# Linear attention's state as (phi(k)^T x) Wv, with phi(k) of all tokens kept and its sum made by GpSimd

## The chip, the cores and the metric

The kernel runs on one core of one Trainium2 chip. The metric is the device time of one launch in microseconds (us). The kernel before takes 493.31 us, the median of three runs (493.12 to 495.45).

## The reference

x is [2048, 1024] in bf16, with 32 heads of 32. Two attention blocks read the same x, and a gate mixes them per token:

```python
g = sigmoid((x * gate_w).sum(-1, keepdims=True))

# A: linear attention
q, k, v = split(x @ A_wqkv)
pq, pk = phi(q), phi(k)              # phi(t) = where(t > 0, t + 1, exp(t)) + 1e-6
kv  = einsum("bhsd,bhse->bhde", pk, v)        # the state: 32 x 32 for each head
z   = einsum("bhsd->bhd", pk)
num = einsum("bhqd,bhde->bhqe", pq, kv)
den = einsum("bhqd,bhd->bhq", pq, z)[..., None] + 1e-6
a   = (num / den) @ A_wo

# B: softmax over 8 keys, the token's own and those 2, 4, ... 14 back
b = window_attention(split(x @ B_wqkv)) @ B_wo

out = g * a + (1 - g) * b
```

B_x is not used. The state is a sum over all 2048 tokens, so nothing of A's output can be made before the last token's phi(k) is there.

## The kernel before

**Order of the work.** The builder writes down operations (engine, cost, what they read and write), and a planner (`Prog.schedule`) puts them in a fixed order for each engine before anything runs: it always takes the ready operation that was written down earliest, with costs that are written in the source. The chip then follows these orders; semaphores carry what one engine waits for from another. The planner runs six times and keeps the order that it finds shortest. In its model every engine works by itself. DMAs are started from SyncE (SP), in order.

**Stages.** Tokens are held in 16 tiles of 128, the even tokens first and then the odd ones, since the window of B steps by two.

1. B's values for all tokens (32 groups), stored to HBM. A *group* is 8 matmuls of 128x512 that fill one PSUM bank (L1323).
2. The gate.
3. B's q and k, transposed, into `qT` and `kT` (64 groups).
4. The *linear phase*: for each tile t, two groups of A's k and two of A's v. k goes through `phi` (L1327 to L1333): ScalarE's exp into `e` (L1329), VectorE's min and add on `e` (L1330), VectorE's max and add from PSUM (L1332). v is moved to SBUF by ScalarE or VectorE, whichever the planner finds free (`move`, L1347). The state of a tile is a *state burst* of 32 small matmuls (L1535: K = 128 tokens, 32 columns, N = 33, the 33rd column being ones, which gives z), and VectorE adds it to `kva` in SBUF (L1543).
5. *Fills*: the window attention of B runs inside stages 3 and 4, one fill of 112 or 114 tokens for every five groups (`slot(FILL)`, 18 fills in all). A fill is a scores burst (L1424), ScalarE's exp into `E` (L1430), VectorE's multiplication by the window's mask (L1433), and a values burst (L1443 and L1449) with its division: ScalarE's Ln and Exp (L1458, L1459), VectorE's product into `qT` (L1460). The scores and values share four PSUM banks; the groups have the other four.
6. `fold`: A's output matrix is multiplied by the state, head by head (L1573), in place in `ws[1]`. `z_spread` copies z to all partitions by two matmuls with ones (L1583).
7. For each tile: `query` (A's q and its phi), `scaled` (VectorE: q times z, sum per head, reciprocal, product; a DMA transposes the result into `kT`, L1610), and `output` (32 matmuls of 128x512, B's and A's part in one bank, L1626).

**SBUF.** `ws` are four weight slots of 16 KB per partition. Slot 1 and 2 hold B's Wk and Wq in stage 3, slot 3 A's Wk and slot 0 A's Wv in stage 4, slot 1 A's Wo and slot 2 A's Wq after that, slot 3 B's Wo.

**Around the change.** The linear phase is one loop over t with four groups each (L1545 to L1563). `states` holds a tile's state burst back by four slots. After the loop, the first queries follow, then `z_spread`, `scaled` and `fold` among queries and the first output (L1637 to L1666).

Of the kernel before, what the change touches and what calls it, by code (L numbers as in the profile page):

```python
# [7 lines left out]
ALU = mybir.AluOpType  # L8
AX = mybir.AxisListType
BF16 = mybir.dt.bfloat16  # L10
# [1092 lines left out]
def build_kernel(nc, A_x, A_wqkv, A_wo, B_x, B_wqkv, B_wo, gate_w, out):  # L1103
# [20 lines left out]

    rings = []
# [40 lines left out]
    ident = SB([128, 128], BF16, "ident")  # L1166
# [11 lines left out]
    kva = SB([128, 8, 33], F32, "kva")  # L1178
    kvb = SB([128, 8, 32], BF16, "kvb")
    kvT = SB([128, 8, 32], BF16, "kvT")  # L1180
    zdg = SB([128, 8, 128], BF16, "zdg")
# [5 lines left out]
    warm = SB([128, 512], BF16, "warm")  # L1187
    er = Ring([SB([128, 512], BF16, "e%d" % i) for i in range(3)])
# [16 lines left out]
    pk = Ring([SB([128, 1024], BF16, "pk%d" % i) for i in range(2)])  # L1205
    az = Ring([SB([128, H, 33], BF16, "az%d" % i) for i in range(2)])
# [3 lines left out]
    pnr = Ring([SB([128, 1024], BF16, "pn%d" % i) for i in range(2)])  # L1210
    base[0] = max(base[0], top_)
    pr = Ring([SB([128, 1024], BF16, "p%d" % i) for i in range(3)])
# [12 lines left out]
    def plan(seen):  # L1225
# [28 lines left out]
        C("pool", lambda e: e.memset(ident[:], 0.0), 0.2, [ident.all()])  # L1254
        C("pool", lambda e: e.affine_select(out=ident[:], in_=ident[:], compare_op=ALU.not_equal, fill=1.0, base=0,
                                            pattern=[[-1, 128]], channel_multiplier=1), 0.3, [ident.all()], [ident.all()])
# [211 lines left out]
        states = []  # L1468

        def slot(rate):  # L1470
            slot_n[0] += 1
            while later and later[0][0] <= slot_n[0]:
                later.pop(0)[1]()
            while states and states[0][0] <= slot_n[0]:
                states.pop(0)[1]()
# [42 lines left out]
        load_w(1, 0, Ao, 0, 40)  # L1518
        load_w(1, 1, Ao, 512, 41)
        load_w(2, 0, Aw, 0, 42)  # L1520
        load_w(2, 1, Aw, 512, 43)


        for z in az.t:
            P.op("pool", lambda e, z=z: e.memset(z[:, :, 32:33], 1.0), 0.2, writes=[z.part((0, H), (32, 33))])

        def state(t, pkt, azt):
            bank = main.next()

            def fn(e):  # L1530
                last = None
                for i in range(8):
                    for j in range(4):
                        h = 4 * i + j
                        last = e.matmul(bank.ap()[32 * j:32 * j + 32, i * 33:i * 33 + 33], pkt[:, h * 32:(h + 1) * 32], azt[:, h, :],  # L1535
                                        start=True, stop=True, tile_position=(0, 32 * j))
                return last
            P.op("pe", fn, 0.22, mode="c", reads=[pkt.all(), azt.all()], writes=[bank.iv], name="kv")
            src = lambda: bank.ap(0, 264).rearrange("p (i c) -> p i c", c=33)
            if t == 0:  # L1540
                P.op("dve", lambda e: e.tensor_copy(kva[:, :, :], src()), dps(264), reads=[bank.iv], writes=[kva.all()])
            else:
                P.op("dve", lambda e: e.tensor_tensor(kva[:, :, :], src(), kva[:, :, :], ALU.add), dps(264), reads=[bank.iv, kva.all()], writes=[kva.all()])  # L1543

        for t in range(NT):  # L1545
            pkt, _ = pk.next()
            azt, _ = az.next()
            xs, xr = x_tile(t)
            for r in range(4):
                bank = main.next()  # L1550
                w, wr = w_half((3, 0)[r // 2], r % 2)
                group(bank, xs, w, [xr, wr])
                if r < 2:
                    phi(bank, pkt[:, r * 512:(r + 1) * 512], pkt.part((r * 512, (r + 1) * 512)))
                else:
                    hh = (r - 2) * 16
                    dst = azt[:, hh:hh + 16, 0:32]
                    src = lambda bank=bank: bank.ap().rearrange("p (h d) -> p h d", d=32)
                    reg = azt.part((hh, hh + 16), (0, 33))
                    move(dst, src, 512, bank, reg)  # L1560
                if r == 3:
                    states.append((slot_n[0] + 4, lambda t=t, pkt=pkt, azt=azt: state(t, pkt, azt)))
                slot(FILL)  # L1563

        def fold(gq, jh):
            bs = [main.next() for _ in range(4)]
            w = ws[1].part((4 * gq, 4 * gq + 4), (jh * 512, jh * 512 + 512))

            def fn(e):
                for a in range(4):  # L1570
                    for j in range(4):
                        b = (a + j) % 4
                        last = e.matmul(bs[j].ap()[32 * b:32 * b + 32, :], kvT[32 * j:32 * j + 32, 4 * gq + b, :], ws[1][32 * j:32 * j + 32, 4 * gq + b, jh * 512:(jh + 1) * 512],  # L1573
                                        start=True, stop=True, tile_position=(32 * j, 32 * b))
                return last
            P.op("pe", fn, 0.45, mode="r", reads=[kvT.all(), w], writes=[b.iv for b in bs], name="fold")
            for j in range(4):
                move(ws[1][:, 4 * gq + j, jh * 512:(jh + 1) * 512], bs[j].ap, 512, bs[j], ws[1].part((4 * gq + j, 4 * gq + j + 1), (jh * 512, jh * 512 + 512)))

        def z_spread():  # L1580
            for hf in range(2):
                bank = main.next()
                P.op("pe", lambda e, hf=hf, bank=bank: e.matmul(bank.ap(), ones[:, :], zdg[:, 4 * hf:4 * hf + 4, :].rearrange("p i n -> p (i n)"), start=True, stop=True),  # L1583
                     mm(512), reads=[ones.all(), zdg.part((4 * hf, 4 * hf + 4), (0, 128))], writes=[bank.iv], name="z")
                move(zb[:, hf * 512:(hf + 1) * 512], bank.ap, 512, bank, zb.part((hf * 512, (hf + 1) * 512)))

        def query(t, r):
            p_ = pr.t[t % len(pr.t)]
            xs, xr = x_tile(t)
            bank = main.next()  # L1590
            w, wr = w_half(2, r)
            group(bank, xs, w, [xr, wr])
            phi(bank, p_[:, r * 512:(r + 1) * 512], p_.part((r * 512, (r + 1) * 512)))

        def scaled(t):
# [8 lines left out]
            for gq in range(2):  # L1604
# [5 lines left out]
            P.op("sp", lambda e: e.dma_start_transpose(kT[:, :, t * 128:(t + 1) * 128], pn[:, :]), 1.5, reads=[pn.all()],  # L1610
                 writes=[kT.part((0, 8), (t * 128, (t + 1) * 128))], chan="pn%d" % (t % 2), lat=1.3)

        def output(t, between=()):
            between = list(between)
# [3 lines left out]
            for f0, f1 in parts:  # L1618
# [4 lines left out]
                for lh, w, first in ((qT, ws[3], True), (kT, ws[1], False)):  # L1623
# [4 lines left out]
                    if not first and between:  # L1628
                        between.pop(0)()
# [7 lines left out]
        for t in range(2):  # L1637
            for r in range(2):
                query(t, r)
                slot(FILL)  # L1640
        while todo or later or states:
            slot(1.0)
        load_w(3, 0, Bo, 0, 50)
        load_w(3, 1, Bo, 512, 51)
        main = Pool(banks)
        P.op("dve", lambda e: e.tensor_copy(kvb[:, :, :], kva[:, :, 0:32]), 0.3, reads=[kva.all()], writes=[kvb.all()])
        P.op("dve", lambda e: e.transpose(kvT[:, :, :].rearrange("p i d -> p (i d)"), kvb[:, :, :].rearrange("p i d -> p (i d)")), 0.3, reads=[kvb.all()], writes=[kvT.all()])
        P.op("dve", lambda e: e.tensor_tensor(zdg[:, :, :], ident[:, None, :].to_broadcast([128, 8, 128]), kva[:, :, 32:33].to_broadcast([128, 8, 128]), ALU.mult),
             1.3, reads=[kva.all(), ident.all()], writes=[zdg.all()])
        query(2, 0)  # L1650
        query(2, 1)
        z_spread()
        scaled(0)
        query(3, 0)
        query(3, 1)
        fold(0, 0)
        output(0, [lambda: fold(1, 0), lambda: (scaled(1), query(4, 0), fold(0, 1), query(4, 1), fold(1, 1), scaled(2))])
        query(5, 0)
        query(5, 1)
        for t in range(1, NT):  # L1660
            if t + 2 < NT:
                scaled(t + 2)
            output(t)
            if t + 5 < NT:
                query(t + 5, 0)
                query(t + 5, 1)  # L1666
# [66 lines left out]
```

## Time and profile before

| | |
|---|---|
| median of 3 runs | 493.31 us (493.12 to 495.45) |
| profiled execution, its own time | 493.83 us |
| its span, first to last instruction | 490.9 us |
| TensorE busy | 477.2 us |
| VectorE / ScalarE / GpSimd busy | 288.5 / 150.8 / 5.1 us |
| granted TensorE clock | 1.00 |
| DMA moved | 39.09 MB |

A row of a timeline has the start in us from the span's start, the duration in us, the engine (PE is TensorE, PEld its weight loads, DVE VectorE, ACT ScalarE, POOL GpSimd), the source line, the operation, its output and input, the shape and how many were merged; in brackets, the idle time before it and what ended that. A row of a group gives the summed busy time, the mean in ns of one, and the idle time before. A row of waits gives the waiting engine and line, what it waited for, the total in us, how often, and the longest. Dense matmuls overlap: one has a duration of 379 ns, but the next starts about 215 ns after it, so the costs of work on TensorE are read from start to start. A few matmul records can be missing from a trace, so a count of x15 can stand for 16.

### The profile page before, as it was taken

How to read it: one execution, taken by the hardware profiler on the slowest of the kernel's cores; microseconds unless marked ns; L12 is line 12 of the kernel's file. 1: busy time of each engine (PE TensorE's matmuls, PEld its weight loads, DVE VectorE, ACT ScalarE, POOL GpSimd, SP SyncE). 2: the span in 40 equal slices, each digit the busy share in tenths (PEclk: the TensorE clock that was granted, in tenths of full speed). 3: DMA queues.
4: the chain of work that ended last, by engine and by line, in shares of the span. 5: the costliest groups of instructions: out<-in, count | busy, mean ns of one | idle time of the engine just before them, and what ended most of it. 6: DMA issues, size and time to landing. Idle time of an engine off the chain costs nothing.

```text
span 490.9 us, 11311 instructions
## 1 busy us (share of the span) xinstructions
PE 477.2 (97%) x5066; PEld 227.7 (46%) x5131; DVE 288.5 (59%) x486; ACT 150.8 (31%) x234; POOL 5.1 (1%) x27
## 2 busy tenths in 40 slices
PE   8999999999999999999999999999999999999996
PEld 3444444444444444455554545444444444444444
DVE  2122144655677777555664654579997777767522
ACT  2111111111344445466565556435322100011000
POOL 4000000000000000000000000000000000000000
PEclk9999999999999999999999999999999999999999
DMA  8989991000005045111100100501233311122111
GB/s 220 218 192 283 347 345 4 1 0 0 2 26 194 23 135 88 40 25 36 35 24 23 29 21 1 163 12 23 64 80 85 52 43 44 43 75 55 43 44 46
DMA packets 64176, 39.09 MB, mean 80 GB/s; under 512 B 39029, under 2 KB 59894, under 8 KB 64122
## 3 DMA queue, kind: packets, MB, share of 16 engines
q1 hardware_dynamic: 63578, 37.78, 29.3%
q8 instruction: 42, 0.69, 0.6%
q10 hardware_dynamic: 544, 0.52, 0.4%
q14 instruction: 12, 0.10, 0.1%
HBM read 21.51 MB, written 8.40 MB: 61 GB/s over the span
## 4 chain that ended last, share of the span: by engine, by line
PE 95%; SPq 2%; issue 2%; DMA 1%; DVE 0%
PE ps_all L1323 65%; PE ps_all L1626 22%; PE ps_all L1424 2%; PE ps_all L1443 2%; SPq L1293 1%; PE ps_all L1535 1%; DMA w<-in_B_wqkv_dram 1%; PE ps_all L1449 1%; SPq L1298 1%; PE ps_all L1387 0%; PE ps_all L1573 0%; DVE o L1353 0%; PE ps_all L1583 0%
## 5 line engine op out<-in xcount | busy, mean ns | idle before, releaser
L1323 PE MATMUL ps_all<-w,xT 128*128 128x512 bf16 x986 | 222.5, 379 | 6.0 <-issue 4.6
L1323 PEld LDWEIGHTS ps_all<-w,xT 128*128 128x128 bf16 x1024 | 97.2, 98 | 117.5 <-issue 2.0
L1323 PE MATMUL ps_all<-xT,w 128*128 128x512 bf16 x497 | 109.9, 379 | 1.7 <-issue 1.4
L1323 PEld LDWEIGHTS ps_all<-xT,w 128*128 128x128 bf16 x512 | 49.3, 98 | 58.8 <-issue 0.4
L1329 ACT ACTIVATE e<-ps_all 128x512 bf16<-128x512 f32 x64 | 38.2, 597 | 124.0 <-PE ps_all L1323 119.7
L1626 PE MATMUL ps_all<-w,kT 128*128 128x512 bf16 (+1 forms) x260 | 60.1, 372 | 0.2
L1626 PE MATMUL ps_all<-w,qT 128*128 128x512 bf16 (+1 forms) x256 | 59.8, 372 | 0.5 <-issue 0.2
L1330 DVE TENSOR_SCALAR e<-e 128x512 bf16<-128x512 bf16 x64 | 18.6, 290 | 40.8 <-ACT e L1329 40.5
L1626 PEld LDWEIGHTS ps_all<-w,kT 128*128 128x128 bf16 x264 | 25.8, 98 | 29.4
L1626 PEld LDWEIGHTS ps_all<-w,qT 128*128 128x128 bf16 x264 | 25.6, 98 | 29.6 <-issue 0.5
L1353 DVE TENSOR_SCALAR o<-ps_all,gm 128x512 bf16<-128x512 f32 (+1 forms) x28 | 20.5, 732 | 27.8 <-PE ps_all L1626 27.8
L1350 DVE CAST vst<-ps_all 128x512 bf16<-128x512 f32 x15 | 10.4, 692 | 43.9 <-PE ps_all L1323 43.9
L1430 ACT ACTIVATE E<-ps_all 128x1824 bf16<-128x1824 f32 (+1 forms) x18 | 30.4, 1687 | 11.7 <-PE ps_all L1424 11.0
L1279 DVE TENSOR_TENSOR mx<-mx,qT 128x1024 bf16<-128x1024 bf16 x32 | 20.7, 688 | 15.3 <-ACT qT L1354 15.2
L1279 DVE TENSOR_TENSOR mx<-mx,kT 128x1024 bf16<-128x1024 bf16 x32 | 20.7, 688 | 14.6 <-ACT kT L1351 14.6
L1433 DVE TENSOR_TENSOR E<-E,msk 128x1824 bf16<-128x1824 bf16 (+1 forms) x18 | 19.8, 1101 | 11.2 <-ACT E L1430 11.2
L1460 DVE TENSOR_TENSOR qT<-ps_all,L 128x456 bf16<-128x456 f32 (+1 forms) x36 | 21.1, 625 | 8.4 <-ACT L L1459 7.9
L1351 ACT ACTIVATE vst<-ps_all 128x512 bf16<-128x512 f32 x17 | 10.1, 597 | 47.9 <-PE ps_all L1323 47.9
L1332 DVE SCALAR_TENSOR_TENSOR pk<-ps_all,e 128x512 bf16<-128x512 f32 x32 | 22.0, 689 | 0.9
L1332 DVE SCALAR_TENSOR_TENSOR p<-ps_all,e 128x512 bf16<-128x512 f32 x32 | 21.7, 686 | 0.8
L1605 DVE TENSOR_TENSOR pn<-p,den 128x512 bf16<-128x512 bf16 x32 | 21.5, 684 | 0.3
L1458 ACT ACTIVATE L<-ps_all 128x456 f32<-128x456 f32 (+1 forms) x36 | 17.8, 547 | 12.4 <-PE ps_all L1443 12.4
(66 smaller groups left out, 247.3 us busy)
## 6 DMA issues: line engine op xcount, KB each, us to landing
w<-in_A_wqkv_dram SPq DMA_DIRECT2D x6, 1024.0 KB, 7.9
v<-vB_hbm SPq DMA_DIRECT2D x36, 128.0 KB, 2.8
vB_hbm<-vst SPq DMA_DIRECT2D x32, 128.0 KB, 5.3
w<-in_B_wqkv_dram SPq DMA_DIRECT2D x4, 1024.0 KB, 8.6
out_dram<-o SPq DMA_DIRECT2D x15, 256.0 KB, 2.1
w<-in_A_wo_dram SPq DMA_DIRECT2D x2, 1024.0 KB, 5.2
w<-in_B_wo_dram SPq DMA_DIRECT2D x2, 1024.0 KB, 6.9
w<-in_B_wqkv_dram SPq DMA_DIRECT2D x6, 256.0 KB, 4.4
```

Source lines behind the costliest of these rows:

```text
L1279: P.op("dve", lambda e, m=m, op=op: e.tensor_tensor(m[:, 0:n], m[:, 0:n], src, op), 0.08 + n / 1920.0, reads=[m.all(), reg], writes=[m.all()],
L1323: last = e.matmul(bank.ap(), lhs(dc), rhs(dc), start=(dc == 0), stop=(dc == 7))
L1329: P.op("act", lambda e: e.activation(e_[:, :], bank.ap(), ACT.Exp), act(512), reads=[bank.iv], writes=[e_.all()])
L1330: P.op("dve", lambda e: e.tensor_scalar(e_[:, :], e_[:, :], 1.0, 1e-6, op0=ALU.min, op1=ALU.add), 0.25, reads=[e_.all()], writes=[e_.all()])
L1332: P.op("dve", lambda e: e.scalar_tensor_tensor(out=dst, in0=bank.ap(), scalar=0.0, in1=e_[:, :], op0=ALU.max, op1=ALU.add), dps(512), read ...
L1353: fd = lambda e: e.tensor_scalar(dst, src(), scale, None, op0=ALU.mult)
L1430: P.op("act", lambda e: e.activation(E[:, 0:32 * nq].rearrange("p (j q) -> p j q", j=4), ps[:, 4:8, 0:8 * nq], ACT.Exp), act(32 * nq), rea ...
L1433: P.op("dve", lambda e: e.tensor_tensor(ev(), ev(), m[:, :, :].rearrange("p r q -> p (r q)")[:, None, :].to_broadcast([128, 16, 2 * nq]), ...
L1458: P.op("act", lambda e, L=L, pb=pb: e.activation(L[:, :, 0:4 * nq], pb(1), ACT.Ln), act(8 * nq), reads=[SO[2].iv, SO[3].iv], writes=[L.all()])
L1460: P.op("dve", lambda e, L=L, pb=pb, g=g: e.tensor_tensor(qT[:, 4 * g:4 * g + 4, t0 + qs:t0 + qs + 2 * nq].rearrange("p c (h q) -> p h c q" ...
L1605: P.op("dve", lambda e, gq=gq: e.tensor_tensor(pn[:, gq * 512:(gq + 1) * 512].rearrange("p (j a d) -> p j a d", j=4, a=4), p_[:, gq * 512: ...
L1626: last = e.matmul(bank.ap(0, f1 - f0), lh[:, k, t * 128:(t + 1) * 128], w[:, k, f0:f1], start=(first and k == 0), stop=(not first and k == 7))
```

## The change

The state is written as kv^T = Wv^T (x^T phi(k)), so A's v is never made.

- The linear phase makes only k: phi(k) of all tokens is kept in `pkS` (32 KB per partition, where slots 1 and 2 were). GpSimd sums its tiles in f32 in `zacc`: one copy and 15 adds of 128x1024.
- Then M = x^T phi(k): x comes a second time from HBM, untransposed, in four column tiles `xn` (two in SBUF at a time, two loads of 512 KB each), and for every 128 columns and each half of phi(k) 16 matmuls of 128x512 sum over all tokens in one bank. M goes to `mT`, in slot 3.
- The state is one burst of 256 small matmuls: for each head 8 of them, over the 1024 inputs, with Wv (slot 0) as weights and M as the moving side. It comes out transposed as `fold` wants it, so the cast and the transpose on VectorE go, as do the 16 state bursts and accumulations and the identity matrix.
- z: GpSimd splits each half of `zacc` into a bf16 high part and a bf16 low part, and `z_spread` is two matmuls for each half, among M's groups.
- The fills go on between M's half groups (8 matmuls each).
- A's Wq goes into the first half of `kT` and A's Wo into its second half (`Half`) as soon as the fills have read them; `fold` works there. The transposed result of `scaled` goes to `aT`, in place of `pkS`; B's Wo into slot 0 behind the state burst.
- After the fills: queries, with the four folds and `scaled` between, then for every tile `scaled`, `output`, `query`.

```diff
+    pkS = SB([128, NT, 1024], BF16, "pk", at=ws[1].lo)
+    aT = SB([128, 8, S], BF16, "aT", at=ws[1].lo)
+    mT = SB([128, 8, 1024], BF16, "mT", at=ws[3].lo)
+    ws += [Half(kT, 0), Half(kT, HS)]
...
+        xns = [load_xn(0), load_xn(1)]
+        aq = []
+        for t in range(NT):
+            xs, xr = x_tile(t)
+            for r in range(2):
+                bank = main.next()
+                w, wr = w_half(3, r)
+                group(bank, xs, w, [xr, wr])
+                if not aq and len(todo) < len(FILLS):
+                    aq.append(load_w(4, 0, Aw, 0, 50))
+                    aq.append(load_w(4, 1, Aw, 512, 51))
+                phi(bank, pkS[:, t, r * 512:(r + 1) * 512], pkS.part((t, t + 1), (r * 512, (r + 1) * 512)))
+                slot(FILL)
+            src = pkS.part((t, t + 1), (0, 1024))
+            if t == 0:
+                P.op("pool", lambda e: e.tensor_copy(zacc[:, :], pkS[:, 0, :]), 2.0, reads=[src], writes=[zacc.all()])
+            else:
+                P.op("pool", lambda e, t=t: e.tensor_tensor(zacc[:, :], zacc[:, :], pkS[:, t, :], ALU.add), 2.5, reads=[src, zacc.all()], writes=[zacc.all()])
+
+        def z_spread(hf):
+            c = slice(hf * 512, (hf + 1) * 512)
+            P.op("pool", lambda e: e.tensor_copy(zh[0][:, :], zacc[:, c]), 1.0, ...)
+            P.op("pool", lambda e: e.tensor_tensor(zh[1][:, :], zacc[:, c], zh[0][:, :], ALU.subtract), 1.3, ...)
+            bank = main.next()
             def fn(e):
+                for i in range(2):
+                    last = e.matmul(bank.ap(), ones[:, :], zh[i][:, :], start=(i == 0), stop=(i == 1))
+                return last
...
+        for c in range(8):
+            tl = xns[c // 2]
+            cs = (c % 2) * 128
+            for r in range(2):
+                bank = main.next()
+                for t0 in (0, NT // 2):
+                    def fn(e, bank=bank, t0=t0, tl=tl, cs=cs, r=r):
+                        for t in range(t0, t0 + NT // 2):
+                            last = e.matmul(bank.ap(), tl[:, t, cs:cs + 128], pkS[:, t, r * 512:(r + 1) * 512], start=(t == 0), stop=(t == NT - 1))
+                        return last
+                    P.op("pe", fn, NT // 2 * mm(512), ...)
+                    if t0:
+                        move(mT[:, c, r * 512:(r + 1) * 512], bank.ap, 512, bank, ...)
+                    slot(FILL)
+                    late_w()
+            if c in (2, 4):
+                z_spread(c // 2 - 1)
+            if c % 2 == 1 and len(xns) < 4:
+                xns.append(load_xn(len(xns)))
...
+        def state():
+            bank = main.next()
             def fn(e):
                 for i in range(8):
+                    for c in range(8):
+                        for j in range(4):
+                            h = 4 * i + j
+                            last = e.matmul(bank.ap()[32 * j:32 * j + 32, i * 32:i * 32 + 32], ws[0][:, c, h * 32:(h + 1) * 32], mT[:, c, h * 32:(h + 1) * 32],
+                                            start=(c == 0), stop=(c == 7), tile_position=(0, 32 * j), skip_group_check=True)
                 return last
+            P.op("pe", fn, 2.1, mode="c", reads=[ws[0].all(), mT.all()], writes=[bank.iv], name="kv")
+            move(kvT[:, :, :].rearrange("p i d -> p (i d)"), lambda: bank.ap(0, 256), 256, bank, kvT.all())
-        def state(t, pkt, azt):
...
-                        last = e.matmul(bank.ap()[32 * j:32 * j + 32, i * 33:i * 33 + 33], pkt[:, h * 32:(h + 1) * 32], azt[:, h, :],
...
+        queries(0)
+        state()
+        load_w(0, 0, Bo, 0, 54)
+        load_w(0, 1, Bo, 512, 55)
+        query(1, 0)
+        query(1, 1)
+        fold(0, 0)
...
```

More of the change, by code (lines that the diff above doesn't have):

```diff
@@ L1528, in state @@
+        def z_spread(hf):
+            c = slice(hf * 512, (hf + 1) * 512)
+            P.op("pool", lambda e: e.tensor_copy(zh[0][:, :], zacc[:, c]), 1.0, reads=[zacc.all()], writes=[zh[0].all()])
+            P.op("pool", lambda e: e.tensor_tensor(zh[1][:, :], zacc[:, c], zh[0][:, :], ALU.subtract), 1.3, reads=[zacc.all(), zh[0].all()], writes=[zh[1].all()])
             bank = main.next()
             def fn(e):
-                last = None
-                for i in range(8):
[L1533 to L1536, printed above, removed]
@@ L1537, in fn @@
-                return last
[L1538 to L1563, printed above, removed]
+                for i in range(2):
+                    last = e.matmul(bank.ap(), ones[:, :], zh[i][:, :], start=(i == 0), stop=(i == 1))
@@ L1577, in fold @@
             for j in range(4):
[L1578 to L1585, printed above, removed]
+                move(ws[5][:, 4 * gq + j, jh * 512:(jh + 1) * 512], bs[j].ap, 512, bs[j], ws[5].part((4 * gq + j, 4 * gq + j + 1), (jh * 512, jh * 512 + 512)))
         def query(t, r):
@@ L1622, in output @@
                 tt = (t * 128, (t + 1) * 128)
-                for lh, w, first in ((qT, ws[3], True), (kT, ws[1], False)):
+                for lh, w, first in ((qT, ws[0], True), (aT, ws[5], False)):
                     def fn(e, bank=bank, f0=f0, f1=f1, lh=lh, w=w, first=first):
@@ L1635, in output, with queries @@
                          reads=[o_.part((c, f1))], chan="out%d_%d" % (os_, c), lat=1.0)
-        for t in range(2):
+        def queries(t):
             for r in range(2):
                 query(t, r)
[L1640 to L1649, printed above, removed]
+        queries(0)
[5 more added lines that the diff above has]
+        fold(0, 0)
         query(2, 0)
+        scaled(0)
         query(2, 1)
-        z_spread()
-        scaled(0)
+        fold(1, 0)
         query(3, 0)
         query(3, 1)
[L1656 to L1660, printed above, removed]
+        fold(0, 1)
+        scaled(1)
+        query(4, 0)
+        query(4, 1)
+        fold(1, 1)
+        for t in range(NT):
             if t + 2 < NT:
```

71 lines of the change are left out of this document (41 added, 30 removed).

## The prediction

> **What bounds the kernel now.** I read the page first (busy times, slices, chain), then the waits of TensorE, then its timeline.
>
> ```profile
> span 490.9 us, 11311 instructions
> ...
> PE 477.2 (97%) x5066; PEld 227.7 (46%) x5131; DVE 288.5 (59%) x486; ACT 150.8 (31%) x234; POOL 5.1 (1%) x27
> ...
> PE 95%; SPq 2%; issue 2%; DMA 1%; DVE 0%
> ```
> ```profile
> PE ps_all L1323 <- issue: 6.0, 38, 0.2
> PE ps_all L1358 <- DVE warm L1271: 1.3, 1, 1.3
> PE ps_all L1323 <- DMA xT<-in_A_x_dram: 0.8, 2, 0.6
> PE ps_all L1626 <- issue: 0.2, 1, 0.2
> ```
>
> The reader is to see that TensorE is busy 97% of the span, is 95% of the chain that ended last, and past the start waits for no other engine. The 38 waits "issue" of 0.16 us are the exits from the tiled bursts. GpSimd does nothing after the masks. So time changes in two ways only: by TensorE work removed or added, or by a new wait in front of TensorE. The sum is made against the profiled execution, 493.83 us (span 490.9, 2.9 outside it), which lies 0.5 above the median of 493.31.
>
> **Part 1: TensorE's work.** The 256 dense matmuls of V become 256 dense matmuls of x^T phi(k), same shape: no difference. What changes are the small ones.
>
> ```profile
> 128.84 5.13 PE L1323 MATMUL ps_all<-xT,w 128*128 128x512 bf16 x23 [0.16 <-issue]
> 133.90 0.28 PE L1443 MATMUL ps_all<-E,v 64*32 64x57 bf16 x24
> ...
> 134.85 0.38 PE L1323 MATMUL ps_all<-xT,w 128*128 128x512 bf16 x1 [0.16 <-issue]
> ```
> ```profile
> 239.20 0.28 PE L1443 MATMUL ps_all<-E,v 64*32 64x57 bf16 x24
> ...
> 239.92 0.38 PE L1535 MATMUL ps_all<-az,pk 128*32 128x33 bf16 x32
> 240.46 0.38 PE L1323 MATMUL ps_all<-w,xT 128*128 128x512 bf16 x1 [0.16 <-issue]
> ```
> ```profile
> 263.99 1.67 PE L1323 MATMUL ps_all<-w,xT 128*128 128x512 bf16 x7 [0.16 <-issue]
> 265.60 0.38 PE L1535 MATMUL ps_all<-az,pk 128*32 128x33 bf16 x32
> 265.91 3.63 PE L1323 MATMUL ps_all<-w,xT 128*128 128x512 bf16 x15
> 269.47 0.28 PE L1443 MATMUL ps_all<-E,v 64*32 64x57 bf16 x24
> ```
>
> A values burst (L1443) alone holds the dense stream from 133.90 to 134.85, 0.95 us; with a state burst (L1535) behind it from 239.20 to 240.46, 1.26. So a state burst beside another costs 0.31. Alone, from 263.99 to 269.47 (24 dense and one state burst) is 5.48 against 128.84 to 133.90 (24 dense) 5.06: 0.42. In the program's order 13 of the 16 state bursts stand beside a values burst and 3 alone: **removed 13 x 0.31 + 3 x 0.42 = 5.3 us**.
>
> Added is one burst of 256 small matmuls (K = 128, 32 columns, N = 32; the old N was 33). The 32 of L1535 last 0.38 with 0.18 for the last one alone, so they start within 0.20: 6.3 ns each, 256 x 6.3 = 1.6, and 0.1 for the change of tiling (0.31 less 0.20). It stands directly behind the last scores burst, so it adds no exit. The longest run of small ones now is 120, and eight of them now add into the same columns, which no row shows for so short an N. An upper bound is the dearest small matmul of the trace, the scores burst:
>
> ```profile
> 235.01 0.70 PE L1424 MATMUL ps_all<-qT,kT 32*64 32x57 bf16 x64
> 235.87 0.38 PE L1323 MATMUL ps_all<-w,xT 128*128 128x512 bf16 x1 [0.16 <-issue]
> ...
> 328.97 0.59 PE L1583 MATMUL ps_all<-zdg,ones 128*128 128x512 bf16 x2
> 329.40 3.62 PE L1323 MATMUL ps_all<-w,xT 128*128 128x512 bf16 x16
> ```
>
> 0.86 / 64 = 13 ns, x 256 = 3.4 us; a gain is excluded, since the work is new. I take **+1.7**, as L1535 has the same tiling. A rule speaks against this: the Trainium skill, "TensorE: Matmul & The Clock Gate", section "Wait — 56ns, not 53.3ns?", has start-to-start never under about 25 ns however small N is; by it the burst would be 6.4 us and the sum below 4.7 higher. L1535's 6.3 ns contradict it, unless it is meant for each column tile by itself.
>
> z takes four 128x512 matmuls for two (high and low halves). The two of L1583 hold the stream from 328.97 to 329.40: **+0.4**. Net on TensorE: -5.3 + 1.7 + 0.4 = **-3.2 us**.
>
> **Part 2: GpSimd beside VectorE.** Sixteen GpSimd operations on 128x1024 (one copy, 15 adds f32 + bf16) now run while VectorE does phi(k) and the window masks. What happens then is seen in the first microseconds only:
>
> ```profile
> 2.50 0.57 DVE L1268 COPY msk<-mt 64x114 bf16<-64x114 bf16 x1 [0.22 <-POOL mt L1266]
> ...
> 2.65 0.38 POOL L1525 MEMSET az<- 128x32 bf16 x2
> ...
> 5.83 0.28 POOL L1266 TENSOR_SCALAR_AFFINE_SELECT mt<-mt 128x112 bf16<-128x112 bf16 x1
> ...
> 5.92 0.24 DVE L1268 COPY msk<-mt 64x112 bf16<-64x112 bf16 x1 [1.00 <-POOL mt L1266]
> 6.22 0.19 DVE L1268 COPY msk<-mt 64x112 bf16<-64x112 bf16 x1
> ```
>
> The copy takes 0.19 with GpSimd still. Beside GpSimd it ends at 3.07 and 6.16, each 0.04 to 0.05 after GpSimd's end (3.03 and 6.11): VectorE's copy stood still until GpSimd was through. The Trainium skill ("SBUF — State Buffer", who interferes with whom) calls it an exclusive lock held for the whole instruction, against VectorE's two-port modes and its two-input operations when GpSimd reads; the rows agree, as far as copies go.
>
> How long is one add? No row shows it. GpSimd's shapes differ little in these rows:
>
> ```profile
> 4.05 0.53 POOL L1266 TENSOR_SCALAR_AFFINE_SELECT mt<-mt 128x114 bf16<-128x114 bf16 x2
> ...
> L1255 POOL TENSOR_SCALAR_AFFINE_SELECT ident<-ident 128x128 bf16<-128x128 bf16 x1 | 0.3, 292 | 0.0
> ...
> L1266 POOL TENSOR_SCALAR_AFFINE_SELECT mt<-mt 128x112 bf16<-128x112 bf16 x2 | 0.5, 283 | 0.0
> ```
>
> By the slope alone, (292 - 283)/16 = 0.56 ns per element, 1024 elements with 0.2 ahead are 0.8 us; if all were proportional, 0.29/114 x 1024 = 2.6. The pair's 0.53 less 0.29 spaces them 0.24 apart: 2.1 ns per element, 2.2 us. I take 2.2, since an add reads two operands. The Trainium skill's "GPSIMD Engine Reference", table of section 3.1, has 4497 ns for 2048 elements: an estimate of 2.25 here.
>
> Where it hurts: a window fill sends scores to ScalarE (E), E to VectorE (mask), and TensorE's next burst waits for the mask. One fill of before:
>
> ```profile
> 235.11 0.60 ACT L1329 ACTIVATE e<-ps_all 128x512 bf16<-128x512 f32 x1 [1.89 <-PE ps_all L1323]
> 235.78 1.69 ACT L1430 ACTIVATE E<-ps_all 128x1824 bf16<-128x1824 f32 x1
> ```
> ```profile
> 235.74 0.29 DVE L1330 TENSOR_SCALAR e<-e 128x512 bf16<-128x512 bf16 x1 [1.19 <-ACT e L1329]
> 236.07 0.69 DVE L1332 SCALAR_TENSOR_TENSOR pk<-ps_all,e 128x512 bf16<-128x512 f32 x1
> 237.50 1.11 DVE L1433 TENSOR_TENSOR E<-E,msk 128x1824 bf16<-128x1824 bf16 x1 [0.74 <-ACT E L1430]
> ```
>
> Counted from the scores' end (235.71), L1332 ends at 1.05, the mask runs 1.79 to 2.90 and the values burst starts at 3.49. Of that 0.59 I take 0.2 for the handover, so a mask later than 3.3 stops TensorE. The changed order keeps this pattern: scores, 16 dense, values, 24 dense, five phi groups to a fill, an add behind every second. I take L1330 and the mask (SBUF to SBUF, as the copies) to be blocked, L1332 (from PSUM) not.
> - Fill with the add behind the group before last: that L1332 ended one group (8 x 0.215 = 1.73) earlier, so the add runs -0.62 to 1.58; L1330, due at 0.03, ends 1.62; L1332 2.34; mask 3.48; values 3.68: 0.2 late.
> - Fill with the add behind the last group: add 1.11 to 3.31, mask to about 4.4, values 4.6: 1.1 late. If the stream is already late so that E is ready when L1332 ends, the mask goes first and it is 0.2 again.
>
> The order has six such fills, three of each kind: 3 x 0.2 + 3 x (0.2 to 1.1) = 1.2 to 3.9; I take **+2.6**. With adds of 0.8 us both kinds come out in time: 0. With 2.6: 3 x 0.6 + 3 x (0.6 to 1.5) = 3.6 to 6.3.
>
> **Part 3: moved things I cost at nothing.**
>
> ```profile
> w<-in_A_wo_dram SPq DMA_DIRECT2D x2, 1024.0 KB, 5.2
> w<-in_B_wo_dram SPq DMA_DIRECT2D x2, 1024.0 KB, 6.9
> ```
>
> The x tiles (8 loads of 512 KB) land in 5 us by these rows; the first two tiles are asked for before the phase, the others 64 dense (13.8 us) ahead. On SP they and the weights pass the v loads, which have three tiles of their own. Wq goes into kT's first half long before use; the second half of Wo waits for the last scores and is due 1.7 + 56 x 0.215 + 0.95 = 14.7 us later; Bo waits for the state burst and is due over 13 us later. Uncovered, each costs up to its 5 to 7 us. The state burst waits for the last move of M behind 8 dense and a scores burst (2.4 us); one queued mask would cost about 1. TensorE's z waits for GpSimd's last add, copy and subtract with 80 dense, 17 us, between: only adds beyond 5 us would show. The freed VectorE and ScalarE work (16 accumulations, half the moves) was not in TensorE's way.
>
> **Sum:** 493.83 - 3.2 + 2.6 = **493.2 us**.
>
> **Rivals.**
> 1. *GpSimd does no harm* (adds near 0.8 us, or the mask not blocked): 493.83 - 3.2 = **490.7**. For it: VectorE has room, 67 of 118 us in the stretch below; against it: the copies above. Chance 0.25.
>
> ```profile
> 195.00:313.20 118.20, 114.32 (x2494) 59.84 (x2519) 67.06 (x124) 68.06 (x102) 0.00 (x0) 1.00 0.10 25
> ```
>
> 2. *Slower: the adds hold VectorE at every fill.* The place is the mask in front of the values burst; it decides once the six waits sum to more than 3.2 us, and to more than 5.7 for a slower kernel that can be told. With adds of 3 us the two kinds are 1.0 and 1.9 late, and VectorE's backlog no longer clears: per token tile TensorE takes 2 x 1.73 + 0.4 x (0.86 + 0.95) = 4.2 us, VectorE 2 x 0.98 + 0.4 x (1.11 + 2 x 0.63, L1460 below) = 2.9, and an add of 3 on top makes 5.9 where nothing overlaps. 3 x 1.0 + 3 x 1.9 = 8.7 at most; I take 7.5: 493.83 - 3.2 + 7.5 = **498.1**. Chance 0.30.
>
> ```profile
> L1460 DVE TENSOR_TENSOR qT<-ps_all,L 128x456 bf16<-128x456 f32 x32 | 18.8, 626 | 7.6 <-ACT L L1459 7.2
> ```
>
> 3. *The long burst is slow.* L1535 starts four column tiles every 0.20/8 = 25 ns; if the added ones, eight deep into the same columns, went one at a time at that pace, they would take 256 x 25 ns = 6.4 us for 1.7: 493.2 + 4.7 = **497.9**. The skill's rule above amounts to this. Against it: L1535. Chance 0.05.
>
> **How the numbers follow.** The forecast has 0.40 (its own range 491.4 to 496.3). About 0.5%, 2.5 us, is what a measurement of this kernel can tell from no change; the forecast lies within it, rival 1 under it (-0.64%), rivals 2 and 3 over it: faster 0.25, same 0.40, slower 0.35. The range runs from a little under rival 1 to a little over rival 2: 490.4 to 499.0.
>
> **What the profile would show.** Right: no L1535 of 32; a state burst of about 1.7 us behind the last scores; adds of about 2.2 us on GpSimd; in the phi(k) stretch L1330 and mask rows drawn out or starting late, and values bursts on TensorE waiting for the mask, some 2 to 3 us in all. Wrong: such waits near zero or over 6 us; a state burst over 3.4 us; TensorE waiting for a DMA at M, at z for GpSimd, or at the folds.

## The result, and the profile after

The changed kernel takes 498.95 us (median of four runs, 498.39 to 499.82) where the kernel before takes 493.34 (493.12 to 495.45): ratio 1.0106, 95% interval 1.0074 to 1.0137. It is slower by 5.6 us, where no change that can be told was forecast. The profiled execution of after took 498.39 us with a span of 496.7.

From the page of the kernel after (span; busy time, share and instructions of each engine; the chain that ended last, by engine):

```profile
span 496.7 us, 10899 instructions
...
PE 483.5 (97%) x4877; PEld 226.2 (46%) x4877; DVE 287.0 (58%) x455; ACT 148.5 (30%) x231; POOL 41.9 (8%) x43
...
PE 93%; DVE 2%; SPq 2%; issue 1%; DMA 1%; ACT 1%
```

TensorE is still the bound, but its share of the chain fell from 95% to 93%, and VectorE has 2% of it. The waits of TensorE (engine, tile and line, what ended the wait, us in total, times, longest):

```profile
PE ps_all L1607 <- issue: 4.7, 1, 4.7
PE ps_all L1454 <- DVE E L1444: 2.0, 3, 1.3
PE ps_all L1369 <- DVE warm L1282: 1.3, 1, 1.3
PE ps_all L1334 <- DMA xT<-in_A_x_dram: 0.8, 2, 0.6
```

The last two were there before. The first two are new: the state burst (L1607) stood still once for 4.7 us, and three values bursts (L1454) waited for the mask (L1444), 2.0 us in all. TensorE's timeline around the state burst, and the granted clock over it and behind it:

```profile
316.61 0.70 PE L1435 MATMUL ps_all<-qT,kT 32*64 32x56 bf16 x64
317.24 1.95 PE L1607 MATMUL ps_all<-mT,w 128*32 128x32 bf16 x208
323.92 0.56 PE L1607 MATMUL ps_all<-mT,w 128*32 128x32 bf16 x48 [4.73 <-issue]
324.40 3.02 PE L1334 MATMUL ps_all<-kT,xT 128*128 128x512 bf16 x8
327.35 0.27 PE L1454 MATMUL ps_all<-E,v 64*32 64x56 bf16 x24
```
```profile
316.00:324.40 8.40, 3.67 (x324) 2.93 (x321) 2.08 (x3) 2.26 (x2) 0.00 (x0) 0.93 0.38 127
324.40:327.30 2.90, 2.90 (x17) 0.98 (x8) 0.42 (x1) 0.00 (x0) 0.00 (x0) 0.60 0.56 177
```

The first 208 small matmuls start within 1.95 us. Then comes a stop that no other engine ends ("issue"), and the last 48. From 317.24 to 324.40 the burst holds the stream for 7.2 us. Behind it the mean granted clock is 0.60 (the number after the last "(x0)"), and 8 dense matmuls take 2.95 us from start to start instead of 1.82: another 1.1.

By the spans, the account is: -5.3 (16 state bursts gone) + 0.4 (z) + 7.2 (the new burst) + 1.1 (clock) + 2.0 (masks) = +5.4, against +5.8 (490.9 to 496.7). The rows name nothing for the last 0.4. In time the two profiled executions lie only 4.6 apart (493.83 and 498.39): outside the span after spends 1.7 us, before 2.9.

### The profile page after: what moved, and what is told of

Same layout as the page of the kernel before. It is cut to its first block, busy times and chain, and to the rows that moved or that the text cites. A ratio compares the mean times of both kernels' runs of the same rounds, so it can differ in the third digit from the quotient of the medians.

```text
span 496.7 us, 10899 instructions
## 1 busy us (share of the span) xinstructions
PE 483.5 (97%) x4877; PEld 226.2 (46%) x4877; DVE 287.0 (58%) x455; ACT 148.5 (30%) x231; POOL 41.9 (8%) x43
## 4 chain that ended last, share of the span: by engine, by line
PE 93%; DVE 2%; SPq 2%; issue 1%; DMA 1%; ACT 1%
PE ps_all L1334 53%; PE ps_all L1666 22%; PE ps_all L1583 11%; PE ps_all L1435 2%; PE ps_all L1454 2%; SPq L1304 1%; DVE E L1444 1%; DMA w<-in_B_wqkv_dram 1%; PE ps_all L1460 1%; ACT E L1441 1%; SPq L1309 1%; PE ps_all L1607 0%; DVE e L1341 0%; PE ps_all L1398 0%; PE ps_all L1621 0%
## 5 line engine op out<-in xcount | busy, mean ns | idle before, releaser
L1334 PE MATMUL ps_all<-w,xT 128*128 128x512 bf16 x512 | 113.5, 379 | 1.0 <-DMA xT<-in_A_x_dram 0.8
L1334 PEld LDWEIGHTS ps_all<-w,xT 128*128 128x128 bf16 x512 | 48.7, 98 | 60.4 <-DMA xT<-in_A_x_dram 2.2
L1666 PE MATMUL ps_all<-kT,aT 128*128 128x512 bf16 (+1 forms) x264 | 60.5, 373 | 0.0
L1334 PE MATMUL ps_all<-kT,xT 128*128 128x512 bf16 x256 | 59.2, 384 | 0.0
L1583 PE MATMUL ps_all<-pk,xn 128*128 128x512 bf16 x256 | 57.5, 379 | 0.0
L1341 DVE TENSOR_SCALAR e<-e 128x512 bf16<-128x512 bf16 x64 | 29.8, 469 | 24.2 <-ACT e L1340 24.0
L1666 PEld LDWEIGHTS ps_all<-kT,aT 128*128 128x128 bf16 x264 | 25.8, 98 | 29.4
L1334 PEld LDWEIGHTS ps_all<-kT,xT 128*128 128x128 bf16 x256 | 24.9, 99 | 30.6 <-issue 2.0
L1583 PEld LDWEIGHTS ps_all<-pk,xn 128*128 128x128 bf16 x256 | 24.1, 98 | 28.1
L1552 POOL TENSOR_TENSOR zacc<-zacc,pk 128x1024 f32<-128x1024 f32 x15 | 32.9, 2196 | 30.6 <-DVE pk L1343 28.4
L1471 DVE TENSOR_TENSOR qT<-ps_all,L 128x456 bf16<-128x456 f32 (+1 forms) x36 | 21.1, 624 | 19.5 <-ACT L L1470 19.5
L1361 DVE CAST kT<-ps_all 128x512 bf16<-128x512 f32 x23 | 15.9, 690 | 25.2 <-PE ps_all L1334 23.8
L1444 DVE TENSOR_TENSOR E<-E,msk 128x1824 bf16<-128x1824 bf16 (+1 forms) x18 | 22.5, 1249 | 11.2 <-ACT E L1441 11.1
```

The costliest lines, as they stand in the source:

```text
L1334: last = e.matmul(bank.ap(), lhs(dc), rhs(dc), start=(dc == 0), stop=(dc == 7))
L1341: P.op("dve", lambda e: e.tensor_scalar(e_[:, :], e_[:, :], 1.0, 1e-6, op0=ALU.min, op1=ALU.add), 0.25, reads=[e_.all()], writes=[e_.all()])
L1361: fd = lambda e: e.tensor_copy(dst, src())
L1444: P.op("dve", lambda e: e.tensor_tensor(ev(), ev(), m[:, :, :].rearrange("p r q -> p (r q)")[:, None, :].to_broadcast([128, 16, 2 * nq]), ...
L1471: P.op("dve", lambda e, L=L, pb=pb, g=g: e.tensor_tensor(qT[:, 4 * g:4 * g + 4, t0 + qs:t0 + qs + 2 * nq].rearrange("p c (h q) -> p h c q" ...
L1552: P.op("pool", lambda e, t=t: e.tensor_tensor(zacc[:, :], zacc[:, :], pkS[:, t, :], ALU.add), 2.5, reads=[src, zacc.all()], writes=[zacc.a ...
```

## The experiments

The stop has three candidate causes. The theory at first was the load of Wo's second half, which goes on at that moment. The rivals were that TensorE's instructions come too slowly for so many small ones in a row, and that a long accumulating burst is slow by itself. Each ratio below is to the kernel before on the same chip.

**e1: the load moved behind the burst.**

```diff
 def late_w():
     load_w(5, 0, Ao, 0, 52)
-    load_w(5, 1, Ao, 512, 53)
...
-state()
+kv_op = state()
+load_w(5, 1, Ao, 512, 53, after=[kv_op])
```

> Only one thing differs from the changed kernel: the second half of A's output matrix (1 MB) is asked for behind the state burst, not in front of it. In the changed kernel the burst stops for 4.73 us after 208 of its 256 matmuls, the load's data run from 318.0 to 321.7 us, and TensorE's next 16 KB block of instructions starts at 321.5, as they end. Theory (the instruction block queues behind the load on the DMA engines): the stop goes, and with it the clock dip behind it (8 dense matmuls in 3.0 us for 1.9), together 5.9 us: about 493. Rival 1 (the burst is longer than the instructions that are held, and the refill is slow by itself): the stop stays near 4.7, about 499. Rival 2 (256 accumulating matmuls of N = 32 are slow by themselves): the same, 499.

Measured: 496.08 us (495.25 to 498.61), ratio 1.0035 [1.0022, 1.0048]. Its waits, then its timeline:

```profile
PE ps_all L1606 <- issue: 3.0, 2, 2.8
```
```profile
318.58 0.80 PE L1606 MATMUL ps_all<-mT,w 128*32 128x32 bf16 x80
319.57 1.19 PE L1606 MATMUL ps_all<-mT,w 128*32 128x32 bf16 x128 [0.20 <-issue]
323.57 0.52 PE L1606 MATMUL ps_all<-mT,w 128*32 128x32 bf16 x48 [2.81 <-issue]
324.03 3.55 PE L1334 MATMUL ps_all<-kT,xT 128*128 128x512 bf16 x8
```

The stop comes after the same 208 (80 + 128), with no load in flight, and is 2.8 us long instead of 4.7. So the load is worth 1.9 us of it, and the larger part is something else. The theory of the load alone fell. The clock dip is there too: 8 dense matmuls take 3.47 us from start to start. But this profiled execution was the slowest of the eight, and three others had a mean clock of 1.00 over the whole execution and took 495.25 to 495.84, so the dip does not come every time.

**e2: the burst in four pieces of 64**, with 8 dense matmuls or more between them, the load where the change has it.

```diff
-queries(0); state(); load_w(0, ...); query(1, 0); query(1, 1); fold(0, 0); query(2, 0)
+queries(0); state(0, 4); query(1, 0); state(1, 4); query(1, 1); state(2, 4); query(2, 0); state(3, 4)
+load_w(0, ...); fold(0, 0)
```

> The state burst is cut into four of 64 matmuls with query groups (8 dense matmuls, 1.73 us) between; the load of the output matrix stays in front of them. Theory: the instructions that are held (some 550 before the stop) now last longer, since 24 to 40 dense matmuls stand between the pieces, so the load is through before they run out: no stop, no dip, -5.9, and three more entries and exits of a burst at 0.1 to 0.2 each, +0.5: about 493.5. Rival 1 (slow refill): nearly the same here, since dense matmuls use few instructions. Rival 2 (slow accumulation): the burst's 7.2 us are only spread, about 499.

Measured: 496.63 us (495.2 to 498.72), ratio 1.0045 [1.0026, 1.0065]. From its waits and its timeline:

```profile
PE ps_all L1454 <- issue: 1.5, 1, 1.5
PE ps_all L1626 <- ACT kT L1362: 1.4, 1, 1.4
```
```profile
319.20 0.66 PE L1609 MATMUL ps_all<-mT,w 128*32 128x32 bf16 x64
319.79 1.90 PE L1334 MATMUL ps_all<-kT,xT 128*128 128x512 bf16 x8
...
321.90 0.44 PE L1454 MATMUL ps_all<-E,v 64*32 64x56 bf16 x32
323.83 0.22 PE L1454 MATMUL ps_all<-E,v 64*32 64x56 bf16 x8 [1.48 <-issue]
```

The state's pieces now run without a stop, each 0.6 us from start to start (319.20 to 319.79), 2.4 for the four. The stop has moved into a values burst (L1454), which is otherwise the same as before, and is 1.5 us. It comes at the same place in TensorE's sequence: counted from the scores burst, after has 64 + 208 = 272 matmuls ahead of the stop, e2 has 64 + 64 + 8 + 64 + 8 + 64 (24 + 8 + 32 of the values burst), 272 too. So it isn't the accumulation or anything in the state's matmuls: whatever stands behind that instruction waits. (This profiled execution is the fastest of the eight. Four others took 497.4 to 498.7 at a mean clock of 0.997; what they lost, beyond a dip of the clock, no kept trace shows.) The order also sets two folds back to back, which costs a new wait of 1.4 us (the second waits for ScalarE to empty the first's bank).

**e3: the 15 GpSimd adds left out.** The kernel sums only the first token tile into z; all else is the change.

```diff
-else:
-    P.op("pool", lambda e, t=t: e.tensor_tensor(zacc[:, :], zacc[:, :], pkS[:, t, :], ALU.add), ...)
```

> The 15 adds on GpSimd are left out (z is that of the first token tile only; its copy and the split stay), all else as in the changed kernel. Theory (GpSimd's adds hold VectorE's operations from SBUF to SBUF): the three waits of values bursts for the mask (0.52, 1.29 and 0.17 us) go, the mask's longest row falls from 3.0 to 1.1 us and the mean of L1341 from 469 to 290 ns: -2.0, about 497. Rival (the masks are late because phi of two halves stands in a row, not because of GpSimd): the waits stay, about 499. The stop in the state burst stays in both.

Measured: 497.63 us (497.2 to 498.29), ratio 1.0061 [1.0044, 1.0078]. The row of L1454 is gone from the waits; the stop in the burst stands as it did:

```profile
PE ps_all L1605 <- issue: 5.0, 1, 5.0
```

1.0106 less 1.0061 is 0.45%, 2.2 us: the mask waits, and little more. The mean of VectorE's op on `e` (L1341) falls from 469 to 305 ns, so it was GpSimd that drew it out. The adds have nothing to do with the stop.

**e4: e1 with the sum on VectorE** (the copy and the splits too), written into M's loop.

```diff
-P.op("pool", lambda e, t=t: e.tensor_tensor(zacc[:, :], zacc[:, :], pkS[:, t, :], ALU.add), ...)
+P.op("dve", lambda e, t=t: e.tensor_tensor(zacc[:, :], zacc[:, :], pkS[:, t, :], ALU.add), ...)   # in M's loop, two for every three half groups
```

> Both: the load behind the state burst, and the sum of phi(k) (one copy, 15 adds, the splits) on VectorE in the stretch of M, where VectorE is busy 17 of 64 us; nothing on GpSimd. Theory: -5.9 - 2.0 = -7.9, about 491, 0.5% under the kernel before; adds of 1.2 us in front of masks may give back up to 1. Rival 1 of the first run: about 497. If VectorE's adds now hold the masks in the stretch of M: waits there, 493 or more.

Measured: 507.37 us (505.75 to 508.02), ratio 1.0262 [1.0244, 1.0279], the worst of all, where about 491 was expected:

```profile
PE ps_all L1454 <- DVE E L1444: 5.8, 2, 3.0
PE ps_all L1435 <- DVE qT L1471: 2.8, 1, 2.8
PE ps_all L1615 <- issue: 2.7, 1, 2.7
```

The adds are not what TensorE waits for here. The planner drew them forward out of M's stretch into that of phi(k), where they ended by 248.5 us without one mask wait on TensorE; the waits come at the last two fills, which this order sets behind the state burst:

```profile
L1554 DVE TENSOR_TENSOR zacc<-zacc,pk x15: 1214/1217/1224, 192.3 to 247.2; 128x1024 f32<-128x1024 f32 x15
```
```profile
320.86 0.70 PE L1435 MATMUL ps_all<-qT,kT 32*64 32x57 bf16 x64
324.51 0.28 PE L1454 MATMUL ps_all<-E,v 64*32 64x57 bf16 x24 [2.95 <-DVE E L1444]
...
329.32 0.78 PE L1435 MATMUL ps_all<-qT,kT 32*64 32x56 bf16 x64 [2.76 <-DVE qT L1471]
```

With no dense matmuls between scores and values, TensorE waits for the whole of a fill's exp and mask, and then for its division (L1471). So the run prices two late fills, and whether the sum is better on VectorE or on GpSimd stays open; why the planner placed the fills so was not tested. The stop is there as well, 2.7 us with no load in flight, though here after 224 small matmuls: it isn't tied to the number 208.

**e5: e1 with the burst done twice over**, 512 small matmuls in one go.

```diff
-for i in range(8):
+for i in [x % 8 for x in range(16)]:
```

> The state burst is done twice over in one go (512 small matmuls, the second half repeating the first; the sum is doubled, so the output is not the reference's), and the second half of Wo is asked for behind it, as in e1, so that no load lies beside it. Theory (slow refill: TensorE holds some 550 instructions, a small matmul is two, and a block of 256 instructions takes at least 3.5 us to come): the first 208 or so start within 2 us, then come pieces of 128 with a stop of 2.5 to 3.0 us before each: three stops in all (against one in e1), 7.5 to 9 us standing, burst from first to last 11 to 13 us. Rival (one-off: a stop of about 2.8 us caused by the change of tiling, by the accumulation, or by whatever happens once): one stop of about 3 us, burst about 6 us. Rival (the long burst is slow by itself, the matmuls going one at a time at 25 ns): 512 x 25 ns = 12.8 us evenly, with no pieces of quick ones between the stops.

(The second pass starts its sums anew, so it repeats the first one and doubles nothing; the work on TensorE is as the text has it.) Measured, one execution: 503.42 us. Its waits and its timeline:

```profile
PE ps_all L1606 <- issue: 7.0, 3, 2.5
```
```profile
316.80 1.95 PE L1606 MATMUL ps_all<-mT,w 128*32 128x32 bf16 x208
321.29 1.19 PE L1606 MATMUL ps_all<-mT,w 128*32 128x32 bf16 x128 [2.54 <-issue]
324.74 1.22 PE L1606 MATMUL ps_all<-mT,w 128*32 128x32 bf16 x128 [2.26 <-issue]
328.19 0.56 PE L1606 MATMUL ps_all<-mT,w 128*32 128x32 bf16 x48 [2.23 <-issue]
```

Three stops, as the slow refill has it: 7.0 us of standing (7.5 to 9 expected), 12.0 us from 316.80 to the end of the last piece (11 to 13). Pieces of 128 small matmuls come every 3.45 us, and within a piece they run at 8 to 9 ns each. The DMA view of the stretch from 316.80 to 328.20, in 40 slices of 0.285 us, shows what comes in that time: nothing but three transfers of the instruction queue.

```profile
DMA  0000002000000000000200000000000200000000
...
q8 instruction: 3, 0.05, 1.8%
```

Each is 16 KB (0.05 MB for three; 57 GB/s in one slice). By the trace's DMA records they begin at 318.7, 322.4 and 325.9, and TensorE goes on 2.3 to 2.6 us after each; the second and third begin 1.1 to 1.2 us after TensorE took up the piece before. A small matmul is two instructions, itself and its weight load, so a piece of 128 is 256. The Trainium skill ("Runtime: NRT & Kernel Launch", section "Instruction fetch mechanics") has instructions refilled in blocks of 16 KiB or 256 instructions, which agrees with these pieces; that the fetch is hidden because instructions are dispatched more slowly than they are filled in does not hold here: a block of 256 came every 3.45 us and took 1.2 to run.

The same view of after, from 316.80 to 324.50 (slices of 0.19 us), shows the second half of its stop:

```profile
DMA  0000000026969999999989999110000000000000
...
q8 instruction: 1, 0.02, 0.8%
```

The load of Wo fills the engines until 321.6, and in the trace's DMA records the one instruction block of this window begins at 321.5, as the load ends: 4.3 us after the burst began, against 2.0 in e1 (320.6, burst from 318.58). That the block was queued behind the load is the reading of these times; the queue itself isn't shown.

**e7: e2 and e1 together.** Pieces of 64, and the load behind the last of them.

> The state burst cut into four pieces of 64 with 8 dense matmuls between them, as in e2, and the second half of Wo asked for behind the last piece, as in e1. Theory (slow refill plus a load in front of it): neither stop nor clock dip is left; against the changed kernel -3.0 (slow refill), -1.9 (held by the load), -1.2 (clock dip), +0.5 to 0.9 (three more changes of tiling at 0.16 to 0.3): about -5.4, so 494 to 495 where before is 494.4, ratio 0.998 to 1.003. Rival (the two edits cure the same microseconds, so e1 or e2 is already the best): 496, ratio 1.003 to 1.005.

Measured: 493.94 us (493.65 to 495.39), ratio 0.9992 [0.9976, 1.0007]. Over the stretch of the burst, at a clock of 1.00 throughout:

```profile
317.20:323.60 6.40, 5.97 (x294) 3.90 (x285) 3.06 (x5) 3.02 (x5) 0.00 (x0) 1.00 0.02 5
323.60:327.30 3.70, 3.66 (x60) 1.70 (x60) 2.14 (x4) 2.09 (x5) 0.00 (x0) 1.00 0.00 0
```

No stop, no dip. Against the change 1.0106 - 0.9992 = 1.14%, 5.6 us, with 5.4 expected: either edit alone gave 3.0 to 3.5. The kernel is now level with the one before, with 2.0 us of mask waits and 1.4 of the fold in it.

**e8: e7 without the 15 adds** (z from the first token tile alone).

> e7 with GpSimd's 15 adds left out (z is then made of the first token tile alone, so the output is not the reference's). Theory: the mask waits of about 2.0 us go as well, and what is left is the work on TensorE: before less 5.3, plus 1.7 for the burst, 0.4 for z and some 0.6 for three more changes of tiling: -2.6, 491.8 where before is 494.4, ratio 0.993 to 0.996. Rival (the 16 state bursts of before were worth less than 5.3): ratio 0.997 to 1.000 and no waits left.

Measured: 491.65 us (491.43 to 491.92), ratio 0.9941 [0.9923, 0.9959], -2.7 us. The size is as expected; its parts are not quite. The fold's 1.4 us wait and 0.5 more at the first loads were not in the text, nor was the time outside the span, which is about 1.1 shorter than that of before (491.65 - 489.9 = 1.75, against a median of 2.9 in this round). About 1 us of the gain lies in no row. So that the sum comes out at the forecast size is in part luck.

**e9: e7 with every add told to wait for a mask as well**, so that adds start when a mask has just been done.

```diff
-P.op("dve", lambda e: e.tensor_tensor(ev(), ev(), m...[:, None, :].to_broadcast(...), ALU.mult), ...
+last_mask[0] = P.op("dve", lambda e: e.tensor_tensor(ev(), ev(), m...[:, None, :].to_broadcast(...), ALU.mult), ...
...
-    P.op("pool", ... ALU.add), 2.5, reads=[src, zacc.all()], writes=[zacc.all()])
+    P.op("pool", ... ALU.add), 2.5, reads=[src, zacc.all()], writes=[zacc.all()], after=[last_mask[0]])
```

> e7 with each GpSimd add also waiting for the mask that the program put down last before it, so that an add does not start while a mask is due; nothing is left out. Theory (adds hold the mask and phi operations of VectorE in the fills): the waits of the values bursts for the mask fall from 2.0 to 0.5 to 1.0 us, time 492.5 to 493.5 where before is 494.4, ratio 0.996 to 0.999. Rival (the adds come as late as before, because the mask they wait for is already done by then): no difference from e7, ratio within 0.1% of it.

Measured: 492.05 us (491.5 to 492.18), ratio 0.9949 [0.9931, 0.9966]: faster than both kernels, with nothing left out. The mask waits are gone from the list altogether (0.5 to 1.0 us were expected to stay). GpSimd's timeline, and the mask's line (the three numbers are the shortest, the median and the longest in ns):

```profile
213.84 6.54 POOL L1553 TENSOR_TENSOR zacc<-zacc,pk 128x1024 f32<-128x1024 f32 x3 [5.50 <-DVE E L1445]
224.00 4.34 POOL L1553 TENSOR_TENSOR zacc<-zacc,pk 128x1024 f32<-128x1024 f32 x2 [3.62 <-DVE E L1445]
```
```profile
L1445 DVE TENSOR_TENSOR E<-E,msk x18: 1093/1101/1110, 131.3 to 317.2; 128x1824 bf16<-128x1824 bf16 x16, 128x1792 bf16<-128x1792 bf16 x2
```

The adds run two or three in a row behind each mask, and no mask is longer than 1.11 us. The same adds, in the same number, cost next to nothing when they start at the right moment: e8, without them, is 0.4 us faster, and the two intervals overlap.

**e10: e9 with 8 dense matmuls between the first two folds.**

```diff
 fold(0, 0); scaled(0); query(2, 1)
-fold(1, 0); query(3, 0); query(3, 1)
+query(3, 0); fold(1, 0); query(3, 1)
```

> e9 with 8 dense matmuls set between the first and the second fold, and 16 ahead of the third (e9 runs the first two folds back to back; the second there waits 1.4 us for the move of the first out of its bank). Theory (that wait is on the path): -1.4 for the wait, +0.2 to 0.3 for one more change of tiling: about 491.0 where before is 494.4, ratio 0.992 to 0.994 (e9: 0.9949). Rival (the moves of ScalarE and VectorE behind the folds are the limit there, and the wait comes back at the next fold or at the first output): within 0.1% of e9.

Measured: 491.72 us where before is 493.56, ratio 0.9956 [0.9943, 0.997]: no better than e9. The wait came back behind the second fold, where a group waits for VectorE to empty its bank:

```profile
332.94 1.90 PE L1334 MATMUL ps_all<-kT,xT 128*128 128x512 bf16 x8 [1.01 <-DVE p L1343]
```

The rival's figure came in. That the emptying of banks is the limit there, and not the place of one fold, fits this row; no other order was tried.

## Why the prediction was wrong

The forecast was 493.2, the result 498.95: inside the range of 490.4 to 499.0, near its upper end, and outside what was called the likeliest (491.4 to 496.3). That the range still holds it is luck: the upper end was set by rival 2, whose mask waits came to 2.0 us of the 7.5 that it took.

**What failed: the price of the added burst in Part 1.** It was taken as +1.7, with 3.4 as its upper bound, and took 7.2, with 1.1 of slow clock behind it. Both bounds came from bursts of 32 and 64, and a rate that holds over 64 was carried on to 256. The rate itself was the smaller error: 208 in 1.95 us are some 9 ns each for the 6.3 taken, and e2's four pieces cost 2.4 in all. What was left out is that TensorE must also be fed: after 208, which are 272 with the scores burst straight in front of them, it had no instructions. e5 shows that price by itself, 256 instructions for each 3.45 us. The longest run of small matmuls in before's trace is 104 (72 of a values and 32 of a state burst; the prediction has 120), so no row showed it, and the bound of 3.4 was too sure. The prediction's own sign of being wrong, a state burst over 3.4 us, is what the profile shows.

**The second thing that failed: a load "cost at nothing".** Part 3 asked of Wo's second half only when it is due itself, 14.7 us later. It was in time. What it did was to lengthen the stop, by 1.9 of the 4.7 us (e1), and the times of the DMA records say that it held up an instruction block.

**Rival 3** had the right place and 497.9, but with a chance of 0.05 and a mechanism (one matmul every 25 ns) that the rows refute: within a piece the small matmuls start 8 to 9 ns apart, and they came in pieces.

**What held.** The adds: 2.2 us estimated, 2196 ns measured. VectorE's ops from SBUF are drawn out beside them, its ops from PSUM not. The groups of after, then single rows of VectorE and GpSimd:

```profile
L1552 POOL TENSOR_TENSOR zacc<-zacc,pk 128x1024 f32<-128x1024 f32 x15 | 32.9, 2196 | 30.6 <-DVE pk L1343 28.4 <-DVE flag L1524 2.2
```
```profile
L1341 DVE TENSOR_SCALAR e<-e 128x512 bf16<-128x512 bf16 x64 | 29.8, 469 | 24.2 <-ACT e L1340 24.0
L1444 DVE TENSOR_TENSOR E<-E,msk 128x1824 bf16<-128x1824 bf16 (+1 forms) x18 | 22.5, 1249 | 11.2 <-ACT E L1441 11.1
L1343 DVE SCALAR_TENSOR_TENSOR pk<-ps_all,e 128x512 bf16<-128x512 f32 x32 | 22.0, 691 | 1.0
```
```profile
200.33 2.25 DVE L1341 TENSOR_SCALAR e<-e 128x512 bf16<-128x512 bf16 x1
...
212.88 3.01 DVE L1444 TENSOR_TENSOR E<-E,msk 128x1824 bf16<-128x1824 bf16 x1 [0.16 <-ACT E L1441]
```
```profile
200.30 2.12 POOL L1552 TENSOR_TENSOR zacc<-zacc,pk 128x1024 f32<-128x1024 f32 x1 [1.88 <-DVE pk L1343]
...
212.80 2.12 POOL L1552 TENSOR_TENSOR zacc<-zacc,pk 128x1024 f32<-128x1024 f32 x1 [0.95 <-DVE pk L1343]
```

L1341 (0.29 in before) and the mask (1.11) each began a moment after an add and ended after it; L1343, from PSUM, kept its 0.69. The step's size was 2.6, and 2.0 was measured (three fills of the six, 0.2 to 1.3 each; e3: 2.2 in time). That the other three came through free was not foreseen. z, M's x tiles and the folds of the change made no new wait, as said.

**The small items.** The -5.3 of the 16 bursts is borne out only roughly: the spans of before and after close with it to 0.4 us, e8 leaves about 1 us open. The 38 waits "issue" of 0.16 us are not "exits from the tiled bursts", as the prediction read them, but missing records: before has 65 fewer matmuls than weight loads (5066 and 5131), after has all 4877 of both and no such wait. The sum compared like with like, so it did not suffer; the bound of 3.4 did, since the 0.86 us of its scores burst hold one dense matmul without a record (after has 0.63 for the same burst, which would make it 2.5). The time outside the span, taken as the same 2.9, is 1.7 in after (498.39 - 496.7) and 1.75 to 1.8 in e7 to e9; why is open.

## What to carry to other kernels

Price a long run of small instructions by two rates, how fast the engine runs them and how fast they can reach it, and put dense work between the pieces, so that the next instructions have time to come. A load that is itself in time can still be dear if it goes out while another queue needs the DMA engines for a moment. And where GpSimd shares time with VectorE, ask not how much it does but what VectorE has to do just then: the same 15 adds cost 2 us in one order and next to nothing in the other.

## What the runs showed of the hardware

- TensorE stood still after 208 pairs of weight load and matmul in a row (after, e1, e3, e5), in each 272 matmuls behind the start of the scores burst, and after 224 in e4's order. In e5 it then took pieces of 256 instructions, one for each 3.45 us. Bursts of 64 with 8 dense matmuls between ran through (e7, e9); with a load beside them the stop was there still, at the same instruction, but shorter (e2: 1.5 us).
- With a load of 1 MB in flight, the next block of 16 KB went out 4.3 us behind the burst's start, as the load ended, against 2.0 us without one, and the stop was 4.7 us instead of 2.8 (after, e1). That the load held it is read from these times.
- The mean granted clock was 0.60 in the 2.9 us behind the stop of 4.7 us, and 0.54 in the 3.5 us behind one of 2.8 us (e1's profiled execution, below); it stayed at 1.00 in e7, which has no stop, and behind e2's of 1.5 us. The Trainium skill ("TensorE: Matmul & The Clock Gate", section "HAM oscillation — how this bites in real kernels") puts the bound at idle gaps of about 3.4 us; here 2.8 was enough, though not in every execution of e1.

```profile
324.20:327.70 3.50, 3.50 (x40) 1.11 (x39) 0.41 (x1) 0.09 (x1) 0.00 (x0) 0.54 0.67 209
```

- A VectorE op on two SBUF inputs, the mask, is held as long as an add of GpSimd runs beside it: 3.01 us for 1.11.
